# The hand-written order of VectorE, ScalarE, GpSimd and the transfers, drawn up anew from the second stage on

## The chip, the cores and the metric

The kernel runs on one core of a Trainium2 chip. A core has five engines that this case speaks of: TensorE (PE in the profile, with its weight loads as PEld), VectorE (DVE), ScalarE (ACT), GpSimd (POOL) and SyncE (SP, which here only issues DMA transfers). Each engine works through its own list of instructions in order; an instruction whose inputs are not ready holds back everything behind it on its engine. The metric is the device time of one execution in microseconds (us), lower is better.

## What is computed

One transformer block with conditioned layer norms (adaLN), linear attention and a SiLU feed-forward part, all in f32. There are 2048 tokens of 576 features, 32 heads of 18, and 4608 hidden features. The reference, cut to what matters:

```python
mod = (silu(c) @ w_mod).reshape(1, 6, 1, -1)
sa, ca, ga, sb, cb, gb = six rows of mod
h = layernorm(x) * (1 + ca) + sa
q, k, v = split(h @ wqkv)                     # 32 heads of 18
phi = lambda t: where(t > 0, t + 1, exp(t)) + 1e-6
kv = einsum("bhsd,bhse->bhde", phi(k), v);  z = phi(k).sum(tokens)
o = (phi(q) @ kv) / (phi(q) @ z + 1e-6)
x = x + ga * (o @ wo)
h = layernorm(x) * (1 + cb) + sb
x = x + gb * (silu(h @ w1) @ w2)
```

## The kernel before

**Numbers.** TensorE multiplies in a reduced f32 format. To keep f32 accuracy each operand is split into a high and a low part, and three products are summed. ACT makes the high part (a copy or cast), DVE or POOL the low part (a subtraction, `sub_hi`, L126 in the profile). So nearly every matmul waits for a pair "ACT copy, then DVE subtract".

**Stages.** Tokens come in 16 tiles of 128 (`t`), and in 4 blocks of 512 (`tb`). The times are those of the profiled execution.

- *First stage, 0 to about 34 us:* loading, the first layer norm, the column form of `mod`, the splits of wqkv, and the first tiles.
- *Second stage, a loop over the 16 tiles, to about 200 us:* for each tile `k_proj`, `v_proj`, `kv_mm` (L594, which accumulates phi(k)ᵀv in the PSUM tiles `kvp`) and half of the `q_proj`. Beside it x of the next block is normalised (`stats` L183, `finish` with `rstd` on POOL L189, `normalise` L198), and turned: `turn_rows` (L642, L644) rearranges it on POOL, and a transposing DMA (L646) writes it to `raw`. `turn` (L650) then reads one chunk at a time on POOL, ACT modulates it (L204) and makes the high part (L210), DVE the low part (L126). `mod_piece` (L522 and after) multiplies a piece of w_mod, row by row, on DVE; its loads are at L271, those of x at L265.
- *Third stage, about 200 to 275 us:* the sums kv and z are masked (L743 to L749), multiplied with `wo` to one matrix M for all heads (L799; the edges of `wo` that straddle two rows are copied by DMA at L634), and each tile's q is normalised (`q_norm`: L771 to L777, where POOL writes `pn` and copies its tail of 64 columns), transposed (`q_transpose`, L834 and L836), and multiplied with M (`attn_out`, L848). `load_mlp` (L853 to L867) brings and splits the first weights of the MLP. Block by block the second layer norm, the transposes (`turn_chunk_k`, L196, L204, L219, L1115, tail at L891) and the first MLP group follow (`mlp_up` L908 to L912, down L919 and L924).
- *The MLP, to the end:* pairs of blocks are multiplied by a scheme with 7 products in place of 8 (sums of blocks at L1051 to L1059, L1160 to L1162 and L1182). A unit is one group of 256 hidden features for one pair of blocks: `up` (L1346), the values (L1360 to L1367), the splits of the operands `ha` to `he` (L1396, L1400), `down` (L1419), the sums into the result (L1427).

**What sets the order.** The program first emits all instructions. Then `arrange` chains those of each engine in the order of a text, `ORDERS`: a number is the place of an instruction in the program's own order on that engine, `6-7` is a run. The chain adds no waits between engines. It covers the first 2527 instructions of PE, 536 of DVE, 398 of ACT, 168 of POOL and 136 of SP: everything up to the second of the MLP's units, at about 400 us. The remaining units are written in their final order by hand (`PLAN`). The DMA waits and the buffers that are used again follow from the program, not from the texts, except that a buffer with several turns is handed on in the order in which its users stand.

The core of `arrange`:

```python
for part in text.split():
    first, *last = part.split("-")
    for i in traced[int(first) : int(last[0] if last else first) + 1]:
        if before is not None:
            no_wait = mybir.DependencyInfo(mybir.DependencyClass.NoSync, mybir.DependencyReason.DATA)
            tc.add_manual_dep(i, before.name, no_wait, reason="arrange")
        before = i
```

The instructions that the prediction names, by engine and number:

| number | what it is |
|---|---|
| DVE 58, 59, 87 | low parts of v in the second stage (L126, `vx`) |
| DVE 122 | first multiply of the first `mod_piece` (L522) |
| DVE 85, 60, 86, 81, 82 | two other low parts of v (85, 86), one of h (60), two normalisations of x (81, 82) |
| DVE 135; 97, 108, 111 | statistics of a later x tile; low parts ahead of the turned chunks |
| DVE 262; 278 | low part of `wo` (L126); end of phi for a q tile (L339) |
| DVE 304, ACT 218, SP 89 | w2 of the first MLP group: times gb (L866), high part (L867), its load |
| DVE 342 | low part of the turned tail (L126, `hT`) |
| DVE 499 | low part of `ha` of the first unit (L1400) |
| ACT 228 | one of the normalisations ahead of the transposes (L196) |
| POOL 114; 124 | tail copy of `pn` (L777); memset of the tail weights `wtb` (L995) |
| SP 70, 72 | two of the edge copies of `wo` (L634) |

## Time and profile before

| | |
|---|---|
| median of 3 runs | 1139.03 us (1138.95 to 1140.97) |
| the profiled execution | 1139.79 us, of which the span of the trace is 1137.7 us |
| granted TensorE clock | 0.999 of full speed |

The page of the profile gives the busy time of each engine, groups of instructions by line, and the chain that ended last. Answers of the trace give the same for a stretch of the span (windows), who waited for whom (waits), and the instructions in order of time (timeline). A timeline row reads: start and duration in us, engine, line, operation, what it writes <- what it reads, shape and count; in brackets the engine's idle time just before it and what ended that idle time. Consecutive equal instructions are merged into one row.

### The profile page before, as it was taken

How to read it: one execution, taken by the hardware profiler on the slowest of the kernel's cores; microseconds unless marked ns; L12 is line 12 of the kernel's file. 1: busy time of each engine (PE TensorE's matmuls, PEld its weight loads, DVE VectorE, ACT ScalarE, POOL GpSimd, SP SyncE). 2: the span in 40 equal slices, each digit the busy share in tenths (PEclk: the TensorE clock that was granted, in tenths of full speed). 3: DMA queues.
4: the chain of work that ended last, by engine and by line, in shares of the span. 5: the costliest groups of instructions: out<-in, count | busy, mean ns of one | idle time of the engine just before them, and what ended most of it. 6: DMA issues, size and time to landing. Idle time of an engine off the chain costs nothing.

```text
span 1137.7 us, 19243 instructions
## 1 busy us (share of the span) xinstructions
PE 1123.2 (99%) x6973; PEld 1034.7 (91%) x6973; DVE 979.9 (86%) x1543; ACT 537.2 (47%) x1112; POOL 688.2 (60%) x782
## 2 busy tenths in 40 slices
PE   8999999999999999999999999999999999999998
PEld 7899999999998899999999999999999999999998
DVE  6876754778888799999999999999999999999996
ACT  5544353546556454445445444444454444444441
POOL 1323430464714777766775776677667757776786
PEclk9999999999999999999999999999999999999999
DMA  9526310221368876976978869769679787697674
GB/s 281 128 91 168 72 37 10 57 94 69 153 258 321 324 288 255 353 278 254 359 266 314 311 252 355 275 251 366 266 272 341 266 331 295 257 349 272 253 298 157
DMA packets 74558, 272.97 MB, mean 240 GB/s; under 512 B 21468, under 2 KB 37600, under 8 KB 51424
## 3 DMA queue, kind: packets, MB, share of 16 engines
q1 hardware_dynamic: 74452, 271.74, 66.0%
q8 instruction: 56, 0.92, 0.3%
q14 instruction: 38, 0.31, 0.1%
q10 hardware_dynamic: 12, 0.00, 0.0%
HBM read 250.12 MB, written 16.78 MB: 235 GB/s over the span
## 4 chain that ended last, share of the span: by engine, by line
PE 87%; DVE 4%; ACT 3%; DMA 2%; POOL 2%; issue 1%; SPq 1%; DVEq 0%; POOLq 0%; ACTq 0%
PE up L1346 33%; PE down L1419 32%; PE psK L231 10%; PE big L231 5%; PE small L908 2%; PE big L919 1%; PE kvp L594 1%; DMA hT<-in_w_mod_dram 1%; DMA raw<-acc 1%; DVE hT L126 1%; POOL h L650 1%; PE big L834 1%; PE up L1449 1%; PE small L219 1%; PE down L1449 1%
## 5 line engine op out<-in xcount | busy, mean ns | idle before, releaser
L1427 DVE TENSOR_TENSOR acc<-down,acc 128x576 f32<-128x576 f32 x330 | 245.8, 753 | 13.4 <-PE down L1419 4.7
L1346 PE MATMUL up<-hT,w 128*128 128x512 f32 x916 | 239.4, 390 | 0.2 <-DVE f L1365 0.2
L1346 PEld LDWEIGHTS up<-hT,w 128*128 128x128 f32 x916 | 164.5, 188 | 25.2 <-DVE f L1365 0.6
L1381 POOL TENSOR_TENSOR s<-f,f 128x256 f32<-128x256 f32 x66 | 51.7, 783 | 157.9 <-ACT f L1362 157.9
L1419 PE MATMUL down<-w,hb 128*128 128x288 f32 x792 | 120.6, 294 | 0.0
L1419 PE MATMUL down<-w,hc 128*128 128x288 f32 x792 | 120.6, 294 | 0.0
L1419 PEld LDWEIGHTS down<-w,hb 128*128 128x128 f32 x792 | 113.7, 188 | 5.2
L1419 PEld LDWEIGHTS down<-w,hc 128*128 128x128 f32 x792 | 113.7, 188 | 5.1
L126 DVE TENSOR_TENSOR w<-v,w 128x288 fp32r<-128x288 f32 (+1 forms) x170 | 115.2, 685 | 3.6 <-ACT w L1080 2.6
L1427 DVE TENSOR_TENSOR U<-down,U 128x576 f32<-128x576 f32 x132 | 99.5, 754 | 18.3 <-PE down L1419 16.4
L231 PE MATMUL psK<-w,hT 128*128 128x352 f32 (+3 forms) x506 | 105.0, 336 | 1.5 <-ACT hT L210 0.7
L1346 PE MATMUL up<-room,w 128*128 128x512 f32 x348 | 91.1, 390 | 0.2 <-DMA room<-hd 0.2
L1400 POOL TENSOR_TENSOR hc<-s,hc 128x512 fp32r<-128x512 f32 x66 | 90.0, 1364 | 0.5 <-ACT hc L1396 0.5
L1362 ACT ACTIVATE f<-f 128x512 f32<-128x512 f32 x102 | 64.3, 631 | 52.9 <-DVE f L1367 28.4
L231 PEld LDWEIGHTS psK<-w,hT 128*128 128x128 f32 x506 | 81.7, 188 | 8.1 <-ACT hT L210 0.9
L1365 DVE TENSOR_TENSOR f<-up,p 128x512 f32<-128x512 f32 x102 | 69.6, 682 | 12.9 <-PE up L1346 12.0
L1385 POOL TENSOR_TENSOR f<-f,s 128x256 f32<-128x256 f32 x66 | 51.3, 778 | 35.6 <-DVE hb L1400 24.4
L1346 PEld LDWEIGHTS up<-room,w 128*128 128x128 f32 x348 | 62.5, 188 | 9.9 <-issue 0.6
L1088 ACT CAST w<-v 128x288 fp32r<-128x288 f32 x85 | 36.8, 434 | 71.1 <-PE down L1419 63.0
L1419 PE MATMUL down<-w,ha 128*128 128x288 f32 x396 | 63.2, 294 | 0.4 <-DVE ha L1400 0.4
L1419 PE MATMUL down<-w,hd 128*128 128x288 f32 x396 | 63.0, 294 | 0.0
L1419 PE MATMUL down<-w,he 128*128 128x288 f32 x396 | 63.0, 294 | 0.0
(311 smaller groups left out, 2514.1 us busy)
## 6 DMA issues: line engine op xcount, KB each, us to landing
hT<-hd SPq DMA_DIRECT2D x66, 1280.0 KB, 6.1
hT<-hd SPq DMA_DIRECT2D x45, 1024.0 KB, 5.4
room<-hd SPq DMA_DIRECT2D x35, 1280.0 KB, 5.5
room<-hd SPq DMA_DIRECT2D x20, 1024.0 KB, 5.1
v<-in_B_w_dram SPq DMA_DIRECT2D x17, 576.0 KB, 6.4
v<-in_B_w_dram SPq DMA_DIRECT2D x17, 512.0 KB, 7.1
hd<-S SPq DMA_DIRECT2D x6, 1024.0 KB
xt<-in_A_x_dram SPq DMA_DIRECT2D x16, 288.0 KB, 3.8
```

The costliest lines, as they stand in the source:

```text
L126: return V.tensor_sub(lo, full, f32(hi))
L231: T.matmul(ps, xpart(a), wpart(b), start=n == 0, stop=n == len(XW) - 1)
L908: T.matmul(ps, left, right, start=n == 0, stop=n == len(seq) - 1)
L1088: A.copy(self.w2[n][:, 0], src)
L1346: T.matmul(ps, left, right, start=first and m == 0, stop=m == len(seq) - 1, skip_group_check=True)
L1362: A.activation(self.f[i, k], self.f[i, k], AF.Silu)
L1365: V.tensor_add(f, self.bank[bank[1]], self.p1)
L1381: G.tensor_add(self.s[:, 0:1], half(i, 0, 1), half(i, 1, 1))
L1385: G.tensor_sub(half(i, 1, 0), half(i, 1, 0), self.s[:, 1:2])
L1400: eng.tensor_sub(t[:, :, 1, :], src, f32(t[:, :, 0, :]))
L1419: T.matmul(ps[:, p, :HALF], self.a[i, n][:, u, p * P : (p + 1) * P], self.w.w2[n][:, v], start=n in (1, 5, 7, 6) and j == 0, stop=j == 2, ...
L1427: V.tensor_add(dst, ps[:, :, :HALF], dst)
```

## The change

Four of the five texts are rewritten: DVE from its 57th place on, ACT from its 43rd, POOL from its 15th and SP from its 36th. The earlier places and the PE text stay. The instructions, the tiles, the transfers and everything behind about 400 us stay as they are. Of the diff, the lines that hold what the prediction speaks of:

```diff
         "DVE": """
   0 3 2 1 4 6-7 11 8 12-13 9-10 14-16 18 17 5 19-22 30 23-24 28-29 25-27 43 31 44 33-34 36 35 37-38 32 39 41
-  40 42 45-47 50 48-49 67-68 51-53 57 69 62-64 66 55-56 65 58 70 85 71 59-60 88 86 73-74 72 76 75 77-79 122
-  87 61 81-82 80 89 83-84 91 54 90 93-94 96 92 123 98 95 99 132 97 135 101 136 133-134 100 104 102 107 105
...
-  146 125 147 120 126 121 128 131 129 193 150-152 194 153 130 195 154-155 157 127 158 162 176 196 177 161
...
-  220 215 219 221 229-230 225 232-234 236 235 231 237-238 240-241 239 223 242 224 243-244 246-248 245
-  249-250 252-253 226 254 251 228 255 258 256-257 259 261 260 263 266 268 270-271 267 269 264 227 272-273
-  265 262 275-277 274 279 281 280 282-284 278 285-286 288-289 295 290 296 291 297 287 302 306 303 298 307
-  292 299 314-315 300 293-294 308-310 304 323-324 331 311 316-317 332 301 312 318-320 340 325 321 326 322
-  341 313 327 351 328 352 334 362 333 338 330 345 363 343-344 370 335 329 336 339 342 337 349 346 353-355
-  347 356 371 348 380 357-358 305 359-361 364-365 381 369 366-367 398 350 372-373 377-378 399 385 416 374
...
-  458 452 471 469 459 475 483 472 462 477 461 473 478 486 484 463 485 487 495 480 474 488 479 489-490 470
-  465 476 491 468 494 493 481 501 482 492 497 496 500 498 502 507 499 506 505 504 511 508 503 509 512 510
...
+  40 42 45-47 50 48-49 67-68 51-53 57 64 70-71 63 122 55-56 65 69 66 58 62 72 88 59 61 73-79 85 60 86 81-82
+  87 89 80 83-84 123 54 91 90 93 92 132 124 96 98 94 99 135 97 136 101 95 133-134 100 138 104 137 139-141
...
+  218-219 215 221 233 229 232 230 234 231 235-237 240 238 241 224 226 225 242 239 243 246 244-245 247-250
+  252 228 253-254 251 255 258 256 259 263 257 261 260 262 266-271 227 264 272-273 275 265 279 276 274 277
+  280-281 278 284 282-283 285-286 288-289 295 290 296 306 291 297-298 307 314 309 315 308 292 323 287 299
+  293 324 294 310 300 316 331-332 302 301 317-318 311 319 312 320-321 340 313 322 326 325 341 327 351 303
+  328 334 333 352 362 339 343 329 338 345 363 304 335 370 346 336 344 342 371 349 347 337 380 330 305 348
+  354 353 355-356 364 357-358 361 360 365 359 350 369 381 366-367 398 372-373 368 377-378 399 374 385 416
...
+  445 436 438-439 431 440-442 447 443 448-449 455 444 450-451 454 456 446 453 469 457 464 471 458 460 475
+  472 459 467 466 461-462 465 477 473 478 452 485 483-484 486-487 479 495 480 488 490 476 474 491 468 489
+  463 470 494 482 493 481 499 492 496 500 498 497 503 501-502 506 505 504 507-509 515 512 510-511 513 518
...
         """,
         "Activation": """
   0-2 4-6 9 7-8 10 3 11-12 16 19 13-14 18 17 15 21 26 20 27 22-23 29 24 28 25 30-31 35 32-33 36-37 46 48 39
-  47 42 38 50 40 44-45 49 55 58 43 41 59 56 34 57 60 51-53 61 54 62-64 67-68 65-66 71 69-70 74-75 72-73
...
-  196-198 200 199 201 203-204 202 205-208 212 209-210 213-214 217 215 211 216 219-220 224 234 225 221-223
-  239 235 229 227 245 231-233 236-237 226 238 230 240 256 228 241 243 242 249 218 250 246 251 248 247 270
-  253 257 244 272 252 254 266 271 268 267 260 278 264 269 265 263 255 273 262 259 261 293 274-276 281 283
...
-  332-333 329 340 331 334 336-337 347 349 345 348 335 353 338 354 350 355-356 346 352 343 351 359 357 363
...
+  47 42 38 49 44-45 50 58 40 43 34 59 41 55-57 60 51 53 52 61 54 62-63 67-68 65-66 64 71 69-70 74-75 72-73
...
+  189-191 193 195 194 192 197-198 200-201 196 199 203-204 202 206 205 207-208 212-213 209-210 214-215 211
+  216 220 219 224-225 234 221-222 239 223 228 245 235 230 229 233 236 240 217 232 227 231 226 237 241 243
+  242 256 244 270 246 248 218 272 249 251-252 247 250 238 257 266 253-254 267 255 268 278 271 269 263 260
...
+  353-354 345 350 338 343 346 355-356 349 351 359 364 358 357 352 360-361 365 368 371 363 366 370 362 372
...
         """,
         "Pool": """
-  6-7 0 3 8 2 4-5 9-15 17-19 16 20-29 31 30 33 32 35 34 36-41 47 43 42 46 48 45 49 44 50-55 59 58 56-57
-  60-67 70 68-69 74 71-72 77 75 78 81 76 84 82 79 73 87 83 80 85 90 88-89 94 86 91 97 95 100 92-93 98 112 99
-  96 116 101 103-104 102 107 113 108 119 105 117-118 109 111 106 110 114-115 120-123 129-132 125-127 140 128
-  133 139 142 144 124 141 143 145 160 147 135 146 148 134 149-152 137 153-155 162 136 138 157 163 159 156
-  158 165 161 164 166-167
+  6-7 0 3 8 2 4-5 9-15 18-19 16-17 20-29 33 31-32 30 35 34 36-41 43 47 42 46 44-45 48-56 59-60 57-58 61-65
+  73 66-67 70 68-69 74 71-72 77 81 75 78 76 84 82 79 87 80 83 90 85 88 94 86 97 91 89 95 92 100 93 96 112 98
+  101 99 116 103-104 107 113 102 119 105 117 108 114 109-110 106 111 115 120-121 118 122-123 129-131 125 132
+  126 133 140 127 124 139 128 142 144-146 141 135 160 143 162 147-150 138 152-153 151 155 154 157 136 159
+  163 134 158 164 161 156 137 165-167
         """,
         "SP": """
-  0-25 30-31 26 28 27 29 32 43 33-35 44 37 36 38-41 45 42 47 46 48 57 52 58 49-51 53 59-60 54-55 65 56 61
-  63-64 62 67 66 68-69 75 78 76 79-81 73 72 71 70 77 74 88 86-87 82 84 83 89 91 90 85 93 92 95 98 97 94 100
-  99 101 104 102 96 103 107 109-110 106 105 108 111-112 115-116 114 118-119 117 113 122 120 123-124 121 129
-  125-128 131 135 130 132 134 133
+  0-25 30-31 26 28 27 29 32 43 33-34 45 44 35 39 37 36 38 47 40 46 41-42 57 48 53 58 49-52 59-60 54-56 61 63
+  62 64 67-68 66 65 69-70 77 81 71 74 73 80 72 79 78 76 75 86 82 84 83 88 91 90 87 85 92 94 89 93 98 97 96
+  107 95 99 101 100 102-103 110 109 105 104 108 106 111-112 116 115 118 117 119 129 114 113 120 124 121 123
+  125-126 122 127-128 131 135 133 130 132 134
         """,
```

More of the change, by code (lines that the diff above doesn't have):

```diff
@@ new lines @@
+            87 89 80 83-84 123 54 91 90 93 92 132 124 96 98 94 99 135 97 136 101 95 133-134 100 138 104 137 139-141
+            105 107 103 142-143 109 144 102 106 110 108 112 146 111 147 114-115 148 145 125 117 193 149 116 118 113
+            119 126 194 120 127 195 128 196 121 131 150-151 197 199 152 129-130 153-154 198 157 202 158 162 200-201
+            155 203 176 161 159-160 177 165 163-164 156 204 178 170 166 205 169 167 171 168 209 172 206-208 179 173
+            210 174 180 182 181 185 188 183 186-187 184 175 189-190 192 211-212 191 217 213 216 223 214 220 222
@@ L80 @@
+            463 470 494 482 493 481 499 492 496 500 498 497 503 501-502 506 505 504 507-509 515 512 510-511 513 518
+            514 516-517 523 521-522 520 524-530 533 532 519 535 534 531
         """,
@@ new lines @@
+            76 79-80 77-78 83 81-82 84-86 93-94 87 95 88-89 96 90-91 99 97-98 104 100 92 101 105 102 106 108-109 107
+            111-112 103 110 116-117 113-114 118 120-121 119 115 122-124 133 131-132 134 126-127 125 128-129 135 137
+            130 136 141-142 138-139 145-146 140 143-144 147-148 157-158 154-155 159 161 156 160 162-163 150 164
+            166-168 153 169 165 171 170 172-174 151 176-177 175 152 178-179 181 180 182 184-186 183 149 188 187
+            189-191 193 195 194 192 197-198 200-201 196 199 203-204 202 206 205 207-208 212-213 209-210 214-215 211
@@ new lines @@
+            216 220 219 224-225 234 221-222 239 223 228 245 235 230 229 233 236 240 217 232 227 231 226 237 241 243
+            242 256 244 270 246 248 218 272 249 251-252 247 250 238 257 266 253-254 267 255 268 278 271 269 263 260
+            273 262 259 265 261 274-275 293 258 276 281 283 277 264 279 282 284 286 305 285 287 296 280 289 307 301
+            290 288 303 302 304 292 297 299 306 291 298 300 308 294-295 309 311-312 315 313 310 314 316 322-323 317
+            319 318 321 320 324 326 339 342 344 325 327-328 330 332 329 333 336 334 340 347 331 341 335 348 337
@@ L96 @@
+            353-354 345 350 338 343 346 355-356 349 351 359 364 358 357 352 360-361 365 368 371 363 366 370 362 372
+            377 369 373 367 384 376 378 374 379 375 381-382 388 385 383 386-387 380 389 391 394 393 392 395 390 397
+            396
         """,
         "Pool": """
-            6-7 0 3 8 2 4-5 9-15 17-19 16 20-29 31 30 33 32 35 34 36-41 47 43 42 46 48 45 49 44 50-55 59 58 56-57
-            60-67 70 68-69 74 71-72 77 75 78 81 76 84 82 79 73 87 83 80 85 90 88-89 94 86 91 97 95 100 92-93 98 112 99
```

17 lines of the change are left out of this document (2 added, 15 removed).

## The prediction

> **What bounds the kernel now.** I read the page's first lines, then the busy time of each engine in five stretches (columns: PE, weight loads, DVE, ACT, POOL, granted clock, DMA share, GB/s), then who made PE wait.
>
> ```profile
> span 1137.7 us, 19243 instructions
> ...
> PE 1123.2 (99%) x6973; PEld 1034.7 (91%) x6973; DVE 979.9 (86%) x1543; ACT 537.2 (47%) x1112; POOL 688.2 (60%) x782
> ```
>
> ```profile
> 0.00:34.00 34.00, 29.37 (x203) 27.32 (x204) 23.68 (x59) 21.57 (x42) 8.37 (x16) 1.00 0.87 253
> 34.00:78.00 44.00, 42.04 (x282) 39.67 (x282) 33.47 (x72) 21.94 (x44) 15.66 (x15) 1.00 0.40 107
> 78.00:200.00 122.00, 122.00 (x778) 114.57 (x777) 75.82 (x134) 49.92 (x102) 31.00 (x33) 1.00 0.31 74
> 200.00:400.00 200.00, 196.02 (x1320) 182.58 (x1319) 158.69 (x268) 111.08 (x211) 101.17 (x103) 1.00 0.50 184
> 400.00:1119.00 719.00, 719.00 (x4294) 656.37 (x4294) 676.35 (x993) 331.41 (x716) 524.58 (x612) 1.00 0.78 291
> ```
>
> TensorE is busy 1123.2 of 1137.7 us, and its list isn't permuted. The lists that are reach from about 34 us to about 400. From 400 to 1119 PE is busy 719.00 of 719.00 us, so the order there could give nothing, and it isn't touched. From 78 to 200 PE has no hole either. The change can gain only what PE now idles in 34 to 78 (44.00 − 42.04 = 2.0 us) and in 200 to 400 (200.00 − 196.02 = 4.0 us); it can lose anywhere. The waits of PE, first of 34 to 78, then of 200 to 400 (total, times, longest):
>
> ```profile
> PE kvp L594 <- DVE vx L126: 1.0, 2, 0.5
> PE psK L231 <- ACT hT L210: 0.7, 1, 0.7
> PE psK L231 <- DVE hT L126: 0.2, 1, 0.2
> ```
>
> ```profile
> PE small L219 <- ACT H L204: 0.7, 1, 0.7
> PE big L834 <- POOL pn L777: 0.6, 1, 0.6
> PE psK L799 <- DMA a<-raw: 0.5, 1, 0.5
> PE psK L799 <- ACT acc L335: 0.4, 2, 0.2
> PE down L1419 <- DVE ha L1400: 0.4, 1, 0.4
> ...
> PE big L834 <- DVE v L322: 0.2, 1, 0.2
> ...
> PE up L1346 <- DVE f L1365: 0.2, 1, 0.2
> ```
>
> A printed gap understates the delay, as PE's matmuls overlap.
>
> ```profile
> 206.07 3.90 PE L231 MATMUL psK<-wq,hT 128*128 128x288 f32 x28
> ```
>
> Twenty-eight in 3.90 us start about 0.14 apart, while one alone shows about 0.29: each printed gap is worth some 0.15 us more. The rows shown hold 4 and 8 single waits, 1.9 and 3.0 us printed, so about 2.5 and 4.2 us of delay; holes that are too short for the list, or cut above, add some 1.5 to the second.
>
> **The change, part by part.** No instruction is added or removed; the price is only who stands behind whom. Counted from the lists, 405 of DVE's 536 places change, 268 of ACT's 398, 95 of POOL's 168, 75 of SP's 136; the largest shift is 33 places on DVE. I looked up each wait above, and each instruction that moves over more than a few places, by the time at which the trace shows its inputs ready.
>
> *Front, 34 to 78 us.*
>
> ```profile
> 38.08 0.41 DVE L126 TENSOR_TENSOR vx<-psK,vx 128x252 fp32r<-128x252 f32 x1
> ...
> 42.79 0.81 DVE L522 TENSOR_SCALAR tmod<-acc,sc 128x1152 f32<-128x1152 f32 x1
> 43.52 0.23 DVE L126 TENSOR_TENSOR vx<-psK,vx 128x72 fp32r<-128x72 f32 x1
> ```
>
> ```profile
> 46.97 3.47 DMA raw<-acc
> ...
> 53.42 5.19 DMA raw<-acc
> ```
>
> ```profile
> 76.53 0.56 PE L231 MATMUL psK<-w,hT 128*128 128x352 f32 x2 [0.68 <-ACT hT L210]
> 77.33 0.79 PE L231 MATMUL psK<-w,hT 128*128 128x352 f32 x3 [0.24 <-DVE hT L126]
> ```
>
> DVE is full from 34 to 43 us. The vx split at 38.08 (DVE 58), which ends PE's first kvp wait, now stands behind the 0.81 us multiply of mod_piece (DVE 122, today at 42.79) too; less the work that moves back behind it, it ends about 0.75 us later, and so does the next one (59). Further on, 85, 60, 86, 81 and 82 come ahead of the tail split of the next tile (87, at 43.52), which ends 1.9 us later by their lengths; PE takes it up some 0.4 us after its end today and is 0.8 late already, so this is another 0.8. PE is then 1.6 us late at 46. But PE idles at 76.53 and 77.33 for 1.2 us of delay (0.68 and 0.24 printed, plus 0.15 each). That end is set by another chain: rstd on POOL, the copies on POOL, the transposing DMAs (rows 46.97 and 53.42), then five rounds of POOL, ACT and DVE, one for each chunk. SP now issues both loads of w_mod ahead of the transposes instead of between them, which brings the last transpose forward by about 1 us; but DVE takes statistics of an x tile (135) ahead of 97, and 108 and 111 slip by 0.5 to 0.7, which takes it back. So I take that chain as unmoved, and 1.6 − 1.2 = **+0.4** is left. Bounds: 0 (chain earlier by as much), +1.6 (chain 1.2 late too).
>
> *78 to 200 us:* nothing to win. Each PE deadline that I compared has 0.2 us of slack or more after the move; I count **0**, with an upper bound of +1.0 for two new waits like those of 38 us.
>
> *200 to 400 us.*
>
> ```profile
> 203.45 0.59 SPq L634 DMA_DIRECT2D a<-raw  x1
> ```
>
> ```profile
> 205.68 2.00 DVE L126 TENSOR_TENSOR vx<-acc,raw 126x576 fp32r<-126x576 f32 x1
> ...
> 218.11 0.35 DVE L774 RECIPROCAL r<-den 128x32 f32<-128x32 f32 x1 [4.06 <-ACT den L772]
> ...
> 220.92 1.51 DVE L339 SCALAR_TENSOR_TENSOR acc<-e,acc 128x576 f32<-128x576 f32 x1
> ```
>
> - PE's wait for a<-raw ends with the DMA issued at 203.45 (SP 70), the last of nine such copies at 0.6 us each. The new list has it first, and the last of the three that this wait needs (72) one or two copies earlier than 203.45, 0.6 to 0.8 us. One copy ahead of it takes the result of DVE 262 (205.68), which moves into an idle stretch before it. 0.5 + 0.15: **−0.6**.
> - DVE 278 (220.92) moves ahead of the reciprocal at 218.11, into its 4.06 us gap. The v split and the qT split that PE waits for follow 1.5 us earlier: 0.2 + 0.15, and another 0.2 behind it: **−0.55**.
>
> ```profile
> 257.37 0.43 ACT L196 ACTIVATE xn<-acc,nm,rstd 128x64 f32<-128x64 f32 x1
> ```
>
> - This one (ACT 228) is the last ahead of H (L204). It and its like go ahead of the exp and den work. That can bring H forward by 0.43 at most; PE's results, which H reads, come in that time too, so I take **−0.25**. The rest of that wait is H's own length and stays.
>
> ```profile
> 310.12 1.28 POOL L1162 TENSOR_TENSOR H<-H,tq 128x512 f32<-128x512 f32 x1
> 311.35 0.69 POOL L777 COPY pn<-pn 128x64 f32<-128x64 f32 x1
> ```
>
> - The pn tail (POOL 114) copies what POOL itself made many instructions earlier, and stood behind the sums of L1162 (310.12 the last). It now goes ahead of both and of two others: 0.6 + 0.15: **−0.75**. The sums feed casts that come after.
>
> ```profile
> 373.97 0.40 ACT L1396 CAST ha<-f 128x256 fp32r<-128x256 f32 x1
> ```
>
> ```profile
> 379.78 0.41 DVE L1400 TENSOR_TENSOR ha<-f,ha 128x256 fp32r<-128x256 f32 x1
> ```
>
> - The ha split is ready at 374.4 and runs at 379.78; it moves ahead by eight places (−0.55). The two holes before it, for the memset of wtb (POOL 124, ahead by four; under 0.2 printed) and for f at L1365, go too (−0.25, −0.35). All three lie where PE itself would now come 2 us earlier while POOL's weight sums don't, so I count half of 1.15: **−0.6**.
> - The two waits for acc L335 are the length of one ACT step after PE; they stay: 0.
>
> Sum: −0.6 − 0.55 − 0.25 − 0.75 − 0.6 + 0.4 = −2.35, say −2.4 us. The profiled execution took 1139.79 us (2.1 around its span), and would take 1137.4. The median of the runs shown is 1139.03, 0.76 less; off that, **1136.6 us**, 0.21% less. Differences up to 0.2% (2.3 us) can't be told from none here, so the forecast lies at that edge.
>
> *A rule against it.* The sum takes durations from the old places. DVE 262 (205.68) is a 126x576 subtract that lasted 2.00 us:
>
> ```profile
> 195.04 0.75 DVE L126 TENSOR_TENSOR vx<-acc,raw 126x576 fp32r<-126x576 f32 x1
> ```
>
> ```profile
> 205.64 3.34 POOL L786 TENSOR_TENSOR w<-acc,z 128x576 f32<-128x576 f32 x2 [5.35 <-ACT z L765]
> ...
> 372.60 1.02 POOL L1378 TENSOR_TENSOR s<-f 128x256 f32<-128x256 f32 x1 [1.33 <-ACT f L1360]
> ```
>
> Its twin at 195.04, with POOL idle, took 0.75; beside POOL's multiply at 205.64 it took 1.25 more. So a move changes a duration: in its new place 262 would be short, and ha, cast earlier too, falls to about 373 us, beside the POOL sum at 372.60, where it may take up to 1.0 us more. The f at L1365 stands behind it, and the wait that I let go would stay or grow: the three last gains would be nothing instead of −0.6, and the result −1.8. [...]
>
> **The rivals.**
> 1. *Everything clears.* If the transposed x come 1.2 us earlier (front 0), the last three count fully (−1.15) and a part of the holes too short for the list goes (−0.5 to −1.5): −3.8 to −5, 1134.0 to 1135.2. For: each of these inputs is ready long before. Against: the same DVE was 8 places in 10 busy there, and what is pulled ahead pushes something back.
> [...]
> 3. *Slower: the second MLP weight.*
>
> ```profile
> 239.06 1.42 DVE L866 TENSOR_TENSOR raw<-raw,bc_gb 128x1152 f32<-128x1152 f32 x1
> ```
>
> ```profile
> 260.88 1.15 ACT L867 CAST w<-raw 128x1152 fp32r<-128x1152 f32 x1
> ```
>
> ```profile
> 273.60 0.62 PE L908 MATMUL small<-hT,wt 128*128 128x512 f32 x2
> ```
>
> The load of w2 (SP 89) moves from place 88 to 93, behind an x load that waits for a pn product two tiles on; the multiply (DVE 304, at 239.06) from 310 to 342, by what stands ahead of it after 265 us; the cast (ACT 218, at 260.88) now stands ahead of the hT casts that DVE's splits for PE at 272 to 275 need. Today the cast waits for nothing; then ACT stands still from 262.5 to 266.5. I get the tail split (DVE 342) at 272.8 against PE's use at 273.60: 0.8 us of slack. It decides from the point where w2 lands more than 0.8 us later than I take it (260), and each microsecond beyond costs PE one. If it lands 5 to 6 us later, because the x load ahead of it is late as well, PE loses 4 to 5, and with the −2.4 the time is 1140.6 to 1141.6. For: it is the largest new wait that I find. Against: nothing else on SP is late at that place.
> 4. *The list isn't followed,* or rooms are dealt out anew: two-buffer tiles get other partners when the order changes, so waits for free rooms appear that the old trace can't show. Between −1 and +2.
>
> **How the numbers follow.** Forecast (−1.8 to −3.8): 0.38. Everything clears: 0.18. Even, rival 4's middle with it: 0.30. Slower by the w2 chain or rooms: 0.14. Of the forecast's 0.38 some 0.26 lies beyond 2.3 us, so faster 0.44, same 0.45, slower 0.11. The range from 1133.6 (all gains, little given back) to 1140.8 leaves out 0.1 above and 0.05 below.
>
> **What would show it.** Right: no PE wait for pn L777 near 310, for a<-raw near 205 or for ha near 380; the kvp waits near 38 to 46 up to 3 us in all, and the hT wait near 77 down to 0.3 or none; PE's stall-free stretch starts 2 to 3 us earlier. Wrong: PE waits between 78 and 200, for L908 near 273, or the first up wait near 371 grown. A different pace behind 400 us would break the premise that nothing changes there.

## The result, and the profile after

The kernel after takes **1147.06 us** (median of 4 runs, 1146.22 to 1147.63) against 1139.11 us before (4 runs beside them): the ratio is 1.0068 with an interval of 1.0057 to 1.0080. It is 8 us slower. The forecast was 1136.6 with a range of 1133.6 to 1140.8, so its sign and its range were wrong. The profiled execution took 1146.82 us.

The page's first lines, then the busy time by stretch, cut 2 to 8 us later than before as the work is that late (columns as before: PE, weight loads, DVE, ACT, POOL, granted clock, DMA share, GB/s):

```profile
span 1145.1 us, 19237 instructions
...
PE 1124.7 (98%) x6973; PEld 1035.2 (90%) x6973; DVE 979.1 (85%) x1543; ACT 539.9 (47%) x1114; POOL 692.1 (60%) x782
```

```profile
34.00:80.00 46.00, 43.63 (x281) 41.35 (x281) 35.43 (x74) 21.81 (x44) 16.88 (x16) 0.96 0.44 123
80.00:202.00 122.00, 122.00 (x777) 114.41 (x776) 74.39 (x133) 49.66 (x101) 33.14 (x31) 1.00 0.28 66
202.00:408.00 206.00, 198.34 (x1333) 184.58 (x1333) 159.68 (x271) 115.82 (x218) 104.02 (x109) 1.00 0.50 179
408.00:1126.00 718.00, 716.47 (x4276) 653.13 (x4275) 673.98 (x988) 328.85 (x711) 520.93 (x607) 1.00 0.78 291
```

Three things to see. PE idles 7.7 us from 202 to 408, where it was 4.0 in the like stretch before; from 80 to 202 there is still nothing. The granted clock of the front is 0.96, not 1.00. And ACT has 1114 instructions instead of 1112, though none was added to the program. The waits of PE from 202 to 412 (total, times, longest):

```profile
PE big L920 <- DVE hs L127: 1.9, 2, 1.5
PE small L909 <- DVE hT L127: 1.7, 1, 1.7
PE down L1420 <- DVE acc L1428: 1.1, 1, 1.1
PE down L1420 <- POOL hc L1401: 0.9, 1, 0.9
PE big L835 <- DVE qT L127: 0.7, 1, 0.7
```

(Lines of the kernel after stand one below those of before: its text of orders is one line longer.) Of the waits that the change was to end, pn, a<-raw and ha are gone, H's is down from 0.7 to 0.4, and f's is up from 0.2 to 0.4. These five lines are new.

**A ledger of lateness.** PE's list is the same in both kernels, so its n-th instruction can be compared: start in the one trace minus start in the other. The first kvp wait, for instance, in the kernel before:

```profile
38.54 0.72 PE L594 MATMUL kvp<-pk,vx 128*128 128x128 f32 x4 [0.51 <-DVE vx L126]
```

and in the kernel after:

```profile
39.60 0.73 PE L595 MATMUL kvp<-pk,vx 128*128 128x128 f32 x4 [0.89 <-DVE vx L127]
```

39.60 − 38.54 = 1.06 us late there. The same difference at fifteen places, named by their time in the kernel before, for the kernel after and four of the runs below:

| at, us | after | e12_front_cut | e7_late_old | c1_three | g1_gains |
|---|---|---|---|---|---|
| 37.6 | −0.05 | −0.01 | −0.09 | −0.41 | +0.50 |
| 81.5 | +2.13 | +0.14 | +1.45 | +1.60 | +0.70 |
| 130 | +2.22 | +0.14 | +1.57 | +1.69 | +0.70 |
| 224.4 | +0.85 | −0.95 | +0.19 | +0.32 | −0.65 |
| 252.9 | +1.72 | −0.09 | +1.06 | +0.47 | −0.66 |
| 261.5 | +1.33 | −0.47 | +0.67 | +0.08 | −1.04 |
| 282.5 | +1.55 | −0.24 | +0.88 | +0.08 | −1.03 |
| 300 | +3.64 | +2.00 | +2.97 | +1.23 | −1.03 |
| 313 | +2.90 | +2.48 | +2.22 | +1.72 | −1.82 |
| 353.8 | +2.46 | +1.77 | +1.98 | +1.11 | −1.80 |
| 360.3 | +5.06 | +4.44 | +1.99 | +1.12 | −1.77 |
| 380.8 | +3.32 | +2.70 | +1.97 | +1.13 | −2.27 |
| 387.5 | +5.16 | +4.49 | +1.94 | +1.13 | −2.29 |
| 411.2 | +7.01 | +6.34 | +1.94 | +1.12 | −2.30 |
| 1115 | +8.22 | +6.64 | +4.42 | +1.42 | −1.16 |

Read down the second column: +2.2 in the front; from there every fall is a gain (1.37, 0.39, 0.74, 0.44, 1.74: 4.7 us in all) and every rise a new wait (0.87, 0.22, 2.09, 2.60, 1.84, 1.85: 9.5 us). 2.2 + 9.5 − 4.7 = 7.0 at 411, where the reordered part ends. Behind it, where nothing was changed, single DMA waits of 0.2 to 1.0 us (printed) come and go from one execution to the next (1.2 in sum here, 2.5 in the profiled run of e7_late_old, none in that of e5_qt); I put no cause on them.

How far one trace can be trusted shows when the runs below are laid beside it. From 202 to 411 us the steps repeat: in the ten traces whose lists hold the new order at that place, the wait for qT costs PE 0.84 or 0.85 us, and in ten that for hs costs 1.66 or 1.67. The front repeats less well: at 130 the eight traces with the new order's front stand at +1.6 to +2.3, the four with the old one at −1.6 to +0.7. With that and the waits behind 411, the median of a few runs can lie more than a microsecond away from what one trace shows. So the price of a single move in the late stretch is read from the ledger between 202 and 411, and a median that shows more is not put down to the move.

**Where each rise comes from**, in the trace of the kernel after. The wait of 1.5 us for hs, at 284 of the kernel before:

```profile
276.93 0.60 ACT L911 ACTIVATE sl<-small 128x512 f32<-128x512 f32 x1 [1.62 <-PE small L909]
277.55 1.28 ACT L332 ACT_TABLE_LOAD   x1
278.84 0.65 ACT L332 ACTIVATE e<-big 128x576 f32<-128x576 f32 x1
...
281.23 1.28 ACT L911 ACT_TABLE_LOAD   x1
282.53 0.60 ACT L911 ACTIVATE sl<-small 128x512 f32<-128x512 f32 x1
...
286.34 1.60 PE L920 MATMUL big<-w,hs 128*128 128x288 f32 x10 [1.51 <-DVE hs L127]
```

The new order puts the exp and the Relu of a late q tile (ACT 253, 254) between the two SiLUs of one hidden group (ACT 266 and 268). At each of the two changes, from SiLU to exp and back, the trace has a table load of 1.28 us: those at 277.55 and 281.23 are the two instructions more on the page. The second SiLU is late by them and by the work between.

The wait for qT, at 252:

```profile
251.94 0.44 ACT L197 ACTIVATE xn<-acc,nm,rstd 128x64 f32<-128x64 f32 x1 [5.37 <-DVE nm L191]
...
252.50 0.68 ACT L837 CAST qT<-big 128x640 fp32r<-128x640 f32 x1
...
254.17 0.74 PE L835 MATMUL big<-ident,pn 128*128 128x128 f32 x5 [0.69 <-DVE qT L127]
```

This xn is ACT 228, the one that the prediction had pulled ahead for H. It waits 5.37 us for its statistics, and the cast of qT (ACT 235), which ran at 245.23 before, stands behind it.

The wait for hT, at 355:

```profile
354.73 0.93 POOL L1030 TENSOR_TENSOR v<-v,bc_gb 128x288 f32<-128x288 f32 x1 [1.02 <-DMA v<-in_B_w_dram]
354.90 2.47 DVE L127 TENSOR_TENSOR w<-v,w 128x256 fp32r<-128x256 f32 x2
355.62 1.47 POOL L1162 TENSOR_TENSOR S<-S,H 128x512 f32<-128x512 f32 x1
...
358.01 1.17 DVE L127 TENSOR_TENSOR hT<-sl,hT 64x512 fp32r<-64x512 f32 x1
...
359.23 0.72 PE L909 MATMUL small<-hT,wt 128*128 128x512 f32 x2 [1.68 <-DVE hT L127]
```

Two weight splits (DVE 467 and 466) now stand ahead of the low parts that PE needs next. Alone such a split takes 0.41 us; beside POOL's work the two take 2.47.

The waits for hd and hc, at 382 to 386:

```profile
383.85 0.68 DVE L1368 TENSOR_TENSOR f<-up,f 128x512 f32<-128x512 f32 x1
...
391.30 0.81 PE L1420 MATMUL down<-w,hc 128*128 128x288 f32 x4 [0.87 <-POOL hc L1401]
```

The value f (DVE 502, the first row; at 377.37 before) fell behind three splits (497, 503, 501), of which the first waits 1.24 us for ACT; everything that is made of it on ACT and POOL is late with it.

The wait for acc at 405, the last one:

```profile
408.46 2.38 DVE L1401 TENSOR_TENSOR hb<-f,hb 128x512 fp32r<-128x512 f32 x2
408.50 1.78 POOL L1401 TENSOR_TENSOR hc<-s,hc 128x512 fp32r<-128x512 f32 x1 [0.85 <-ACT hc L1397]
...
411.56 1.07 PE L1420 MATMUL down<-w,hd 128*128 128x288 f32 x6 [1.06 <-DVE acc L1428]
```

A split of hb (DVE 531) that ran at 398 in the kernel before stands last in the new list, its cast (ACT 392) late as well. It runs at 409, long beside POOL, and lies ahead of the sum that frees PE's buffer.

The front follows with its runs.

### The profile page after: what moved, and what is told of

Its sections match the earlier page's. It is cut to its first block, busy times and chain, and to the rows that moved or that the text cites. A ratio compares the mean times of both kernels' runs of the same rounds, so it can differ in the third digit from the quotient of the medians.

```text
span 1145.1 us, 19237 instructions
## 1 busy us (share of the span) xinstructions
PE 1124.7 (98%) x6973; PEld 1035.2 (90%) x6973; DVE 979.1 (85%) x1543; ACT 539.9 (47%) x1114; POOL 692.1 (60%) x782
## 4 chain that ended last, share of the span: by engine, by line
PE 87%; DVE 4%; ACT 4%; DMA 2%; issue 1%; POOL 1%; SPq 0%; DVEq 0%; POOLq 0%; ACTq 0%
PE up L1347 32%; PE down L1420 31%; PE psK L232 11%; PE big L232 5%; PE big L920 2%; PE small L909 1%; PE kvp L595 1%; DVE w L127 1%; DMA room<-hd 1%; ACT xn L197 1%; PE small L220 1%; DVE hT L127 1%; PE big L835 1%; PE up L1450 1%; PE down L1450 1%
```

## The experiments

Unless it is said otherwise each starts from the kernel after, and its edit is a part of one engine's text of orders. "PE" means the ledger above, against the kernel before.

### The first three suspects: table loads, weight splits, the front

```diff
 "Activation"
- 238 257 266 253-254 267 255 268
+ 238 257 253-254 266-267 255 268
```

> The new order with one edit on ScalarE: the exp and the Relu of a late q tile (numbers 253 and 254) go ahead of the first SiLU of the first MLP group instead of between its two SiLUs. Theory A (local stalls, each with its own cause; here two extra activation-table loads of 1.28 us each, 277.55 and 281.23 in the trace of the new order, which put off the second SiLU and with it hs): two table loads fewer, the PE wait for hs near 286 (1.51 us printed, 1.8 of delay) goes, about 1.8 us less than the new order, near 1145.2. Rival B (what is late there is late for several reasons, the qT and den steps on ScalarE and VectorE above all, and another wait takes its place): 0.0 to 0.6 us less.

1145.22 us (1143.73 to 1146.19), ratio to before 1.0052 (1.0037 to 1.0067), 1.8 below the kernel after. The page of this run has 1112 ACT instructions again, the wait for hs falls from 1.51 to 0.42 us, and PE is 1.3 us earlier at 300 (+2.29 for +3.64). At 411 it is level again (+7.02): the wait for hT has grown from 1.68 to 2.15, and in this one execution TensorE's clock was at half from 358 to 362. The median is 1.8 lower all the same; how much of that is the edit's, these runs don't tell.

```diff
 "DVE"
- 475 472 459 467 466 461-462 465
+ 475 472 459 461-462 467 466 465
```

> The new order with one edit on VectorE: the two weight splits 467 and 466 (1.04 and 1.51 us long there, 0.41 each when GpSimd is idle) go behind the tail split 462 instead of ahead of the turned chunks 461 and 462. Theory A: they stand for 2.4 us between PE and the tail chunk; the PE wait near 359 (1.68 printed, 1.8 of delay) goes, 1.6 to 1.8 us less than the new order. Rival C (the lengthening by GpSimd falls on whatever VectorE runs in that stretch, so 461 and 462 grow in their place): at most 0.8 us less, and 461 and 462 show over 1.2 us each.

1146.72 us (1145.99 to 1147.76), ratio 1.0067 (1.0052 to 1.0082): nothing. The trace shows why. The wait for hT falls from 1.68 to 0.41, but two others take its place:

```profile
357.48 0.73 PE L909 MATMUL small<-hT,wt 128*128 128x512 f32 x2 [0.41 <-DVE hT L127]
...
363.53 0.50 PE L920 MATMUL big<-w,hs 128*128 128x288 f32 x2 [0.77 <-DVE acc L925]
364.70 3.58 PE L920 MATMUL big<-w,hs 128*128 128x288 f32 x23 [0.67 <-DVE hs L127]
```

The same DVE work has to pass beside the same POOL work; which of PE's operands it delays is all that the one edit changes. So the 2.6 us belong to the order of the whole stretch, not to these two splits.

For the front, the old lists of all four engines up to some place are set ahead of the new ones; the cut is where both hold the same instructions on that engine:

```python
for engine, cut in {"DVE": 90, "Activation": 61, "Pool": 19, "SP": 48}.items():
    order[engine] = before[engine][:cut] + after[engine][cut:]
```

> The new order with the old one up to about 47 us on all four engines (VectorE's first 90 places, ScalarE's first 61, GpSimd's first 19, SyncE's first 48). Theory A: the loss before 77 us (vx waits 1.1 us, and TensorE at half clock from 41 to 44.5 us, 1.3 us) goes, the granted clock stays at 1.00, PE stands where it stands in the kernel before at 78 us, and the end is 2.2 us earlier than in the new order, near 1144.9. Rival D (a late PE at 78 us is what lets the waits at 205 to 224 us be shorter): 0.5 to 1.5 us earlier, with a wait for a<-raw or qT back.

1153.24 us (1150.33 to 1153.74), ratio 1.0125 (1.0108 to 1.0142): 6 us slower than the kernel after. In its trace, which is of the fastest of the four runs, PE is on time at 48.7 (−0.38) with the old front, and 7.8 late at 68. The cut makes a stall of its own:

```profile
52.70 1.42 DVE L525 SCALAR_TENSOR_TENSOR tmod<-acc,sc,tmod 128x1152 f32<-128x1152 f32 x1 [5.81 <-DMA acc<-in_w_mod_dram]
```

The new DVE list takes this multiply early because the new SP list issues its load early; with SP's old head it waits 5.81 us. Lists of several engines are drawn up together, and a mixture of two isn't between them.

```diff
 "DVE" (of the kernel before)
- 55-56 65 58 70 85 71 59-60 88 86 73-74 72 76 75 77-79 122 87
+ 55-56 65 122 58 70 85 71 59-60 88 86 73-74 72 76 75 77-79 87
```

> The kernel before with one edit on VectorE: the first multiply of mod_piece (122, 0.81 us) ahead of the vx split 58. Theory E (the half clock comes from how long PE stood idle between 37 and 41 us): the kvp waits grow by 0.8 us, and if that is enough the granted clock falls to 0.5 for some 3 us right behind: PE 2.1 us later at 46 us, 0.9 later at 78, near 1140.0. If it is not enough: PE 0.8 later at 46, all of it absorbed at 77, 1139.1 as before. Rival F (the half clock has to do with the other moves of the new order): no change of the clock, and no change of the time beyond 0.3 us.

1139.40 us (1138.79 to 1140.56, 10 runs), ratio 1.0001 (0.9991 to 1.0010). In its trace the second kvp wait is 1.28 us for 0.51, so the moved multiply costs PE 0.77 us there, as the prediction has it (0.75); the granted clock stays at 1.00. PE is 0.73 late at 48.7 and still 0.85 late at 300. The absorption at 77 doesn't come, as the chain that ends there moves with DVE (its rstd starts at 44.07, before at 43.06). That is one execution, and the front varies by more than 0.85 us from one to the next; the interval of the median, −1.0 to +1.1 us, holds such a loss as well as none.

### One by one in the late stretch

```diff
 "Activation"
- 239 223 228 245 235 230
+ 239 223 245 235 228 230
```

> The new order with one edit on ScalarE: the normalisation 228, which the new order takes ahead and which waits there for nm (251.94 in its trace), goes behind the qT cast 235. Theory A: the qT cast no longer stands behind a waiting instruction; the PE wait for qT near 254 (0.69 printed, 0.85 of delay) goes, and the 0.3 won at 260 by taking 228 ahead stays: 0.8 us less than the new order. Rival B: H is late again by 0.3, and the late qT has a second cause on VectorE: 0.0 to 0.4 us less.

1145.09 us (1144.47 to 1145.38), ratio 1.0053 (1.0036 to 1.0069). PE is 0.70 earlier at 252.9 (+1.02 for +1.72) and keeps 0.65 to 411. H is no later for it (its wait is 0.43). The median is 2.0 below that of the kernel after; what it shows beyond 0.65 lies behind 411 in the trace (+6.36 here at 1115, +8.22 there).

```diff
 "DVE"
- 500 498 497 503 501-502 506
+ 500 498 502 497 503 501 506
```

> The new order with one edit on VectorE: the value step 502 of the first unit goes ahead of the three weight splits 497, 503 and 501, of which the first waits for ScalarE (382.12 in the trace of the new order). Theory A: the chain value, SiLU, two GpSimd sums, hc cast, hc split comes 1.5 to 2 us earlier, and the PE waits for hd and hc near 386 and 391 (0.28 and 0.87 printed, 1.5 of delay with a third small one) go: 1.2 to 1.5 us less than the new order. Rival B: the splits moved behind it become late for PE, or hc stays late as GpSimd has other work ahead of it: 0.0 to 0.6 us less.

1145.13 us (1144.15 to 1145.87), ratio 1.0053 (1.0038 to 1.0068). PE rises by nothing between 380.8 and 387.5 (+2.93, +2.92), where the kernel after rises by 1.84: the waits for hd and hc are gone. The median is 1.9 below the kernel after.

```python
for engine, cut in {"DVE": 435, "Activation": 325, "Pool": 124, "SP": 113}.items():
    order[engine] = after[engine][:cut] + before[engine][cut:]
```

> The new order up to about 338 us and the old one from there on (VectorE from place 435, ScalarE from 325, GpSimd from 124, SyncE from 113; at each the two lists have held the same instructions). Theory A: PE leaves 340 us 2.9 us later than in the kernel before and loses nothing behind it, as the old order fits there: 4.5 to 5.5 us less than the new order, 1141.5 to 1142.5. Theory G (the waits behind 340 us come from arriving late and with other buffers, whatever the order there): at most 2.5 us less, and the waits for hT near 359 and hc near 391 are still there. By theory A VectorE's lengthening beside GpSimd between 345 and 412 us falls from 8.5 us to the 2.4 of the kernel before.

With the old order from about 338 us on: 1142.30 us (1140.97 to 1144.03, 8 runs), ratio 1.0029 (1.0019 to 1.0040), 4.8 below the kernel after. PE stays at +1.9 to +2.0 from 353 to 411 instead of climbing from 2.5 to 7.0. More than half of the loss is made in the last 70 us of the list. Here the cut makes no stall of its own.

```diff
 "DVE"
- 520 524-530 533 532 519 535 534 531
+ 520 524-526 531 519 530 528 527 532 529 533 535 534
 "Activation"
- 389 391 394 393 392 395
+ 389 391-392 394 393 395
```

> The new order with its last ten places on VectorE as in the old one (the low part of hb, 531, first and not last) and its ScalarE cast 392 right behind the SiLU 391. Theory A: 531, which the new order puts last of all and which takes 1.78 us there beside GpSimd, delays the sum at L1428 behind it, on which PE waits near 411 (1.06 printed, 1.4 of delay); without it 1.2 to 1.4 us less than the new order. Rival B: 531 is late on ScalarE, or the stall moves to hb or ha itself: 0.0 to 0.6 us less.

1146.47 us (1145.76 to 1147.45), ratio 1.0063 (1.0050 to 1.0077). At 411 PE is 5.84 late for 7.01: the wait for acc is gone in the trace, a smaller one of 0.30 stands behind it, and the rise from 387.5 to 411 is 1.00 for 1.85. The median shows 0.6, which four runs can't tell from nothing.

Then e1_table, e5_qt and e7_late_old in one kernel:

> The new order with three of the edits at once: the old order from 338 us on (as in e7_late_old), the exp and Relu ahead of the SiLUs (as in e1_table), the normalisation behind the qT cast (as in e5_qt). Theory A: the three add up, 5.1 + 1.3 + 0.7 us at 412 us by their traces, PE 0.1 us earlier than in the kernel before to 0.5 later there, 1139 to 1140. Rival B (they overlap): 1140.5 or more.

1140.12 us (1138.86 to 1142.65, 10 runs), ratio 1.0009 (1.0000 to 1.0018). It is 6.9 us below the kernel after, where the three alone gave 1.8, 2.0 and 4.8, 8.6 in sum: most of it adds up, and the time lies between the bounds of the two theories. In the ledger the front is left, and a wait for qT of 1.09 us at 313 stands where the gain of pn was.

### The front

Two theories were left: the vx splits make PE late and nothing absorbs it, or the chain of turned chunks, which ends at 77, is late by itself. The second, in the trace of the kernel after:

```profile
63.55 0.46 DVE L184 BATCH_NORM_STATS2 st<-xt 128x6 f32<-128x288 f32 x1 [3.88 <-DMA xt<-in_A_x_dram]
63.93 0.68 DVE L127 TENSOR_TENSOR hT<-h,hT 128x512 fp32r<-128x512 f32 x1
64.67 1.34 POOL L651 COPY h<-raw 128x1024 uint16<-128x1024 uint16 x1 [3.85 <-DVE hT L127]
```

The statistics at 63.55 are DVE 135, which the prediction saw and priced at 0.5 to 0.7. They wait for an x tile; hT (97), whose ACT part is done at 62.32, stands behind, POOL's next copy waits for that hT, and four more rounds follow in lockstep.

First e3's cut without SP's, so that the load of w_mod stays early:

> As the run with the old front (e3_front_old), but SyncE keeps the new order, so that the load of w_mod which VectorE's 123 needs is early. Theory A: PE is as early as in the kernel before at 46 us, no half clock, and 2.0 to 2.2 us earlier than in the new order at 82 us: the end 1.5 to 2.2 us less than the new order. Rival D (the loss of the front is given back later, as a late PE makes later waits shorter): 0.3 to 1 us less. In both the 6 us stall of e3_front_old near 54 us is gone; if it isn't, its cause was not that load.

1146.98 us (1146.38 to 1148.50), ratio 1.0072 (1.0057 to 1.0087). PE is on time at 48.7 (−0.17) and 2.9 late at 68:

```profile
48.78 2.07 DVE L525 SCALAR_TENSOR_TENSOR tmod<-acc,sc,tmod 128x1152 f32<-128x1152 f32 x1 [1.71 <-DMA acc<-in_w_mod_dram]
53.09 0.50 PE L232 MATMUL psK<-w,hT 128*128 128x512 f32 x1 [1.25 <-DVE acc L339]
...
59.00 3.96 PE L232 MATMUL psK<-wq,hT 128*128 128x288 f32 x28 [1.34 <-DVE vx L127]
```

So the vx splits are not all: with them right, the multiplies of the next pieces (123, 124), which the new list has earlier, do the same harm ten microseconds on. In part the mixture makes it: in the kernel after, where DVE comes to 123 later, that multiply starts at 48.73 without a wait.

Then both suspects on DVE alone, the vx splits ahead again and 135 behind 97:

```diff
 "DVE"
- 57 64 70-71 63 122 55-56 65 69 66 58 62 72 88 59 61 73-79 85 60 86 81-82
- 87 89 80 83-84 123 54 91 90 93 92 132 124 96 98 94 99 135 97 136 101 95
+ 57 64 70-71 63 58 122 55-56 65 69 66 59 62 72 88 61 73-79 85-87 60 81-82
+ 89 80 83-84 123 54 91 90 93 92 132 124 96 98 94 99 97 135 136 101 95
```

> The new order with VectorE's front mended in two places: the v splits 58, 59 and 87 go ahead of the work that the new order put before them (60 behind 87), and the statistics 135, which wait for an x tile until 63.5 us, go behind the low part 97 of the turned chunk. Theory A (two chains end near 78 us, PE's own through vx and the turned chunks through 97; each is some 2 us late in the new order): PE is 1.3 to 2.1 us less late at 82 us, no half clock near 42 us, and the end 1.3 to 2.1 us less than the new order. Rival D (another step of the turned chunks is late as well): 0.3 to 1.0 us less.

1147.07 us (1146.00 to 1148.18), ratio 1.0068 (1.0054 to 1.0082): no gain, and PE is 4.6 late at 48.7.

```profile
38.26 0.42 DVE L127 TENSOR_TENSOR vx<-psK,vx 128x252 fp32r<-128x252 f32 x1 [2.42 <-ACT vx L550]
...
41.96 0.47 PE L595 MATMUL kvp<-pk,vx 128*128 128x128 f32 x1 [2.00 <-DVE vx L127]
```

The split needs the high part from ACT (ACT 40), which the new ACT list has four places later (35.23 before, 37.91 after), behind a step that waits 0.63 us for PE. Ahead on DVE alone, it only holds up the DVE. I had read the lateness off the DVE's list and never looked at ACT's.

What was open then: does the front's order make the 2.2 us, or would the stages behind it give the same lateness anyway? This run has all four old lists up to about 130 us, where PE waits for nothing in either kernel:

```python
for engine, cut in {"DVE": 201, "Activation": 131, "Pool": 44, "SP": 69}.items():
    order[engine] = before[engine][:cut] + after[engine][cut:]
```

> The kernel after, with the old order on all four engines up to one common cut at about 130 us (the first 201 places of DVE, 131 of ACT, 44 of POOL, 69 of SP; up to there both orders hold the same instructions on each engine) and the new order behind it. Theory A (the front's 2.2 us are made by the front's order itself, and the parts add up): TensorE stands within 0.5 us of before at 205 us, where the kernel after is 2.2 late, and everything behind shifts with it: 1144.9 us, 2.2 below the kernel after. Theory B (what follows sets the end there: the stages behind 130 us have their own late chain, as with the run that had the old front on four engines but another cut): TensorE is on time at 130 and at least 1.5 us late again at 284, beyond the 1.54 of the table loads, and the time stays at 1146.5 to 1147.5.

1145.08 us (1144.06 to 1145.33, 5 runs), ratio 1.0052 (1.0039 to 1.0064), 2.0 below the kernel after. PE is +0.14 at 130 and −0.95 at 224: the front's order makes the front's loss, as the first theory has it. But the theory's other half, that everything behind shifts with it, fails in the trace: of the 2.1 us that PE is ahead of the kernel after at 130, 0.4 are left at 313 (+2.48 for +2.90) and 0.7 at 411 (+6.34 for +7.01). What the median shows beyond that lies behind 411 again, so that it agrees with the 1144.9 of the theory is in part luck. Most is given back at 313, by a wait that a late PE had hidden:

```profile
306.72 0.76 DVE L849 TENSOR_TENSOR acc<-big,acc 128x576 f32<-128x576 f32 x1 [1.60 <-DMA acc<-in_A_x_dram]
...
313.23 0.81 DVE L127 TENSOR_TENSOR qT<-big,qT 128x640 fp32r<-128x640 f32 x1
...
314.19 0.74 PE L835 MATMUL big<-ident,pn 128*128 128x128 f32 x5 [1.09 <-DVE qT L127]
```

The sum at 306.72 (DVE 403) waits 1.60 us for its x load in this run. In the kernel after it starts at 306.81, where DVE was busy until then (0.06 us idle). So an earlier PE doesn't make it earlier, and the qT split (402) stands eleven places behind it in the new list.

### The gains alone

A few moves in the kernel before and nothing else (ten instructions; the expectations count them as nine moves): those to which the prediction gave a gain, with DVE 497 out of the way of 499, and for H an ACT instruction (238) moved back instead of 228 forward.

```diff
 "DVE"
- 259 261 260 263 266 268 270-271 267 269 264 227 272-273 265 262 275-277
+ 259 261 260 263 262 266 268 270-271 267 269 264 227 272-273 265 275-277
- 274 279 281 280 282-284 278 285-286
+ 274 279 281 280 278 282-284 285-286
- 482 492 497 496 500 498 502 507 499 506
+ 482 492 496 500 498 497 499 502 507 506
 "Activation"
- 226 238 230 240 256 228 241 243 242 249
+ 226 230 240 256 228 241 243 242 238 249
 "Pool"
- 117-118 109 111 106 110 114-115
+ 117-118 114 109 111 106 110 115
- 125-127 140 128 133 139 142 144 124 141
+ 125-127 124 140 128 133 139 142 144 141
 "SP"
- 78 76 79-81 73 72 71 70 77
+ 78 76 72 71 70 79-81 73 77
```

> The kernel before with nine moves and nothing else: GpSimd 114 behind 118 and 124 behind 127, SyncE 72, 71, 70 ahead of 79, VectorE 262 behind 263, 278 ahead of 282, 499 ahead of 502, 497 behind 498, ScalarE 238 behind 242. These are the moves to which the forecast gave its gains of 200 to 400 us (for H at 258 us another ScalarE step is moved out of the way, as the one that the new order moved stalls the qT cast). Theory A (gains and losses are local): the waits for a<-raw, v, H, pn, wtb, f and ha go, PE is 2.5 to 3.2 us earlier than in the kernel before at 412 us: near 1136.3. Rival B (a wait that goes is taken by the next): at most 1.2 us less.

**1135.78 us** (1134.91 to 1137.48, 6 runs) against 1139.04 (16 runs): ratio 0.9967 (0.9955 to 0.9979). PE goes from +0.70 at 130 to −2.30 at 411, 3.0 us. The waits go one by one, for the same amounts as in the kernel after: a<-raw 0.64 us, v 0.35, qT 0.27, H 0.30, pn 0.73, wtb 0.27, ha 0.55, in all 3.1 (f's stays). One part is given back at 360:

```profile
356.27 1.29 POOL L1162 TENSOR_TENSOR H<-H,S 128x512 f32<-128x512 f32 x1
...
356.62 1.50 DVE L126 TENSOR_TENSOR hs<-sl,hs 128x512 fp32r<-128x512 f32 x1 [1.79 <-ACT hs L911]
...
358.04 0.74 DVE L924 TENSOR_TENSOR acc<-big,acc 128x576 f32<-128x576 f32 x1
...
359.47 0.74 DVE L924 TENSOR_TENSOR acc<-big,acc 128x576 f32<-128x576 f32 x1
...
360.36 1.83 PE L919 MATMUL big<-w,hs 128*128 128x288 f32 x12 [0.40 <-DVE acc L924]
```

PE is earlier, hs now falls beside the POOL sum (1.50 us, before 0.83), and the sum into acc that PE waits for (DVE 485, at 359.47) is late by that. Another such sum (484, at 358.04), which was ready earlier, stands between the two. DVE idles 1.79 us ahead of hs, so 484 costs nothing there:

```diff
 "DVE" (of g1_gains)
- 461 473 478 486 484 463
+ 461 473 478 484 486 463
```

> The kernel before with the nine moves of g1_gains and one more: DVE 484 (the take-up of w2's product into acc) ahead of 486 (low part of hs), which lasts 1.50 us beside POOL in g1_gains. Theory A: the wait of TensorE for acc at 360 (0.40 printed, 0.6 of delay) goes, and TensorE, 2.8 us ahead of before by the moves less 0.6 there, keeps it: 1135.2 us, 0.6 below g1_gains. Theory B: the low part of hs itself is then late by the length of 484 (0.74), TensorE waits for hs instead, and the time is that of g1_gains, 1135.8, or up to 0.3 above.

**1135.37 us** (1134.23 to 1136.11, 6 runs) against 1138.98 (10 runs): ratio 0.9968 (0.9956 to 0.9980). PE's wait for acc shrinks to 0.25 (0.40 in g1_gains) and doesn't go, so the working of the first theory isn't borne out: 484 is out of the way, but the split between hs and 485 (wtb) now falls beside a POOL sum and takes 1.50 us for 0.84, so that 485 ends 2.1 us behind hs in both. The seven waits above go for the same amounts again, with PE 2.3 us earlier than in g1_gains from the front on. It is the fastest kernel of this study, 3.6 us faster than before and 11.7 faster than the kernel after; whether the last move adds anything can't be told, as the two medians differ by 0.4 and their runs overlap.

## Why the prediction was wrong, step by step

- **What bounds the kernel** held. Nothing was won or lost from 80 to 202 us, and 7.0 of the 8.2 us of PE's lateness lie where the lists were changed.
- **The old waits, −2.75 us in all, held.** a<-raw and the v and qT splits: −1.15 told, −1.37 measured. H: −0.25 told, −0.39. pn: −0.75 told, −0.74. Of the last three, −0.6 told, two went, ha (−0.55) and wtb (−0.27); f's wait grew by 0.24. The fall of 1.74 that the ledger has there holds two more waits that went (0.36 for a DMA, 0.24 for acc) and small ones, of which the prediction says nothing. g1_gains shows that the gains are real without the rest: 3.0 us in its trace, 3.3 in its median.
- **The front, +0.4 (0 to +1.6), was +2.2**, beyond its upper bound. The 1.6 us at 46 came out as a number (e2_wsplit, with the same front and the full clock, is at +1.71 at 48.7), in part by luck: the first 0.67 us of it is PE's wait for ACT's cast of vx, and the working looked at DVE alone. "I take that chain as unmoved" was the wrong sentence: the last hT of the chain that ends at 77 ran at 78.71 for 76.58, 2.1 late, and 1.6 of that is DVE 135 with its wait for a load ahead of hT (its ACT part was done at 62.32, and it ran at 63.93). I had priced the length of 135 and not what it waits for. So 0.8 us of PE's lateness was absorbed there and not 1.2.
- **The failed step is the sum from 200 to 400.** It holds the waits that the old trace shows, and for all else "each instruction that moves over more than a few places, by the time at which the trace shows its inputs ready". That test looks at an instruction as one that is moved earlier. It doesn't ask what is put *behind* it, nor see an instruction that falls back against work that passes it. So each new wait stood in the sum at nothing. Five of them make up 7.2 of the 9.5 us, and all are of this kind: qT behind an xn that waits (0.84), the second SiLU and with it hs behind an exp (1.5), hT behind two splits (1.8), f and with it hd, hc and he behind three (1.8), a sum behind hb (1.2). The one rival that was of this kind had the wrong place: ACT did wait 4.07 us for the w2 chain, and it cost PE nothing that shows (+1.33 at 261.5, +1.55 at 282.5). The prediction's signs of being right share the blind spot. No wait for pn, a<-raw or ha, the kvp waits under 3 us, the hT wait at 77 down to 0.17: all of these came, and the kernel was 8 us slower, since each watches a place that waited before. The one sign that looks at PE as a whole, a stall-free stretch that starts 2 to 3 us earlier, didn't come.
- **H's xn (ACT 228) is the clearest case.** The prediction took its move as a gain of 0.25 and didn't ask what stands behind it. By its statistics it waits 5.37 us, and qT pays 0.87. e5_qt takes the wait away and keeps the gain.
- **What POOL's work adds to a DVE instruction beside it** was weighed for two places, and it decided more. DVE 262 and 278 became short as told (2.00 to 0.74 us, 1.51 to 0.75). But sum, over every DVE instruction, its time less that of the shortest of its line and shape in the same trace: from 200 to 290 us this lengthening is 13.6 us before and 7.1 after; from 345 to 412 it is 6.0 and 10.7. So the new order takes 6.5 us of it off the DVE in the first stretch, and puts 4.7 on in the second, where PE then waits. e7_late_old has 6.0 there again, and none of the loss. That POOL is behind it shows by kind: in the kernel after, the 331 DVE instructions with two inputs from SBUF that run beside a POOL instruction that reads are 0.36 us longer than their shortest on average, the 253 such that run beside none 0.03, and the 560 with an input from PSUM, POOL beside them too, 0.01.
- **The rivals.** The doubt about the front (+1.6 among the prediction's bounds) was right, and left out the other 9.5 us. "Slower" looked for one large wait and not for five middling ones.

What stays open: how much of the front is the vx casts on ACT and how much the chain behind DVE 135, as no run has the two apart with ACT put right; and why the medians of e5_qt, e6_f and e12_front_cut lie 1.9 to 2.0 us below the kernel after, where their traces at 411 are ahead by 0.65, 2.25 and 0.67.

## What to carry to other kernels

An order is read backward: for each instruction that PE waits for, list what now stands ahead of it on its engine, and ask of each of those what it waits for itself; one early instruction with a late input (the xn here, 5.37 us) holds up everything behind it on its engine. Where a new order gains and loses, line up PE's n-th instruction in both traces: the falls say which moves to keep, and a few of them in the old order gave 3.3 us where the whole new one lost 8. The rises don't simply add up: taking 2.1 us of lateness out of the front uncovered a wait at 313 and left 0.7 at 411. A load of a table of functions (1.28 us here) belongs to the price of an order on ACT, and POOL's neighbourhood to the price of a DVE instruction (0.36 us more on average here, with two inputs from SBUF and beside a POOL instruction that reads).
